# The first 25 microseconds of a four-layer kernel: first tile's mean by halves, transposes reordered, third tile turned by DMA

## The chip, the cores and the metric

The kernel runs on one core of one Trainium2 chip. The metric is the device time of one execution in microseconds (us); lower is better. The kernel before takes 1623.7 us (median of 6 runs).

## The reference

Four layers in turn, A, B, A, B. Only the start of the first one matters here: a layer norm of `x` (2048 x 1024, bf16), then the key, query and value projections.

```python
def _layernorm(x, axis=-1, eps=1e-5):
    m = jnp.mean(x, axis=axis, keepdims=True)
    v = jnp.var(x, axis=axis, keepdims=True)
    return (x - m) / jnp.sqrt(v + eps)
# layer A (cut): qkv = layernorm(x) @ wqkv; linear attention; @ wo; residual
# layer B (cut): ((layernorm(x) @ w_gate) * (layernorm(x) @ w_up)) @ w_down; residual
```

## The kernel before

Rows of `x` are 16 tiles of 128. A tile is centred (the division by the deviation comes later, as the `scale` of an exponential and a relu), transposed so that its 1024 features lie on the partitions, and multiplied with eight slices (128 features each) of the key weights. In the opening, two tiles advance together through the slices as these arrive. A "slice" below is such a piece of weights, 256 KB, as large as a tile of `x`. PE is the engine of matmuls, DVE the vector engine, ACT the scalar engine. To turn a tile is to transpose it, and to evict it is to copy it out of PSUM, where PE has written it.

```python
for c in range(2):                                   # tile 0 in two halves
    load(X[:, 0, c * NB:(c + 1) * NB], x_view[:, 0, c * NB:(c + 1) * NB])
load_x(1)
for k in range(2):    load_k(k, k + 1)               # slices 0, 1
load_x(2)
for k in range(2, 4): load_k(k, k + 1)
load_x(3)
for k in range(4, 8): load_k(k, k + 1)
# ... cut ...
nc.vector.memset(xT[3][:, 0, :], 0.0)
def idle(n):          # n dummy matmuls, 128x512, that keep PE active before data is there
    for _ in range(n):
        nc.tensor.matmul(out=zps[:, 0, :], lhsT=xT[3][:, 0, 0:P], rhs=xT[3][:, 0, :], start=True, stop=True)
# ... cut ...
idle(9)
ln_stats(0)                                          # two bn_stats and an aggregate on DVE
centre(0, stat[0][0][:, 0:1])
nc.scalar.activation(out=junk[:], in_=X[:, 1, :], func=ACT.Copy, scale=1.0 / D, accum_out=mean1[:])
turn_pe(0, 2)                                        # transposes on PE, in two PSUM tiles
take(nc.vector.tensor_copy, 0, 0, 0, 2)              # evict what the first matmul needs
take(nc.scalar.copy, 0, 1, 2, 8)
centre(1, mean1[:])
k_part(0, 0, 1)                                      # tile 0, slice 0: two matmuls
turn_pe(1, 4)
take(nc.vector.tensor_copy, 1, 0, 0, 4)
take(nc.scalar.copy, 1, 1, 4, 8)
ln_stats(2)
centre(2, stat[2][0][:, 0:1])
k_part(1, 0, 1)
for k in range(1, 3):
    for t in range(2): k_part(t, k, k + 1)
turn_pe(2, 8)                                        # tile 2: eight transposes on PE
for t in range(2): k_part(t, 3, 4)
take(nc.scalar.copy, 2, 0, 0, 8)
ln_stats(3); centre(3, stat[3][0][:, 0:1])
turn(XN[:, 3, :], 0, 3)                              # tile 3: turned by DMA
load_q()                                             # query weights, then tiles 4 to 15
# ... cut: the remaining slices of tiles 0 to 2, tile 3, then the queries
```

## Time and profile before

| | before |
|---|---|
| device time, median of 6 | 1623.7 us |
| device time of the traced execution | 1624.31 us |
| PE busy share of the span | 99% |
| named waits of PE, whole run | 2.3 us |
| exponential of tile 3 starts (tiles 0 to 3 done on PE) | 22.20 us |

The page of the profile, its first lines:

```profile
span 1622.4 us, 18054 instructions
PE 1609.2 (99%) x7718; PEld 735.2 (45%) x7869; DVE 615.5 (38%) x941; ACT 283.8 (17%) x383; POOL 54.5 (3%) x135
```

PE does 99% of the span; only what PE does, or waits for, can matter. The view of waits, for PE, shows what it waited for, in us:

```profile
PE ps L168 <- DVE xT L163: 1.2, 1, 1.2
PE pt L411 <- DVE R L398: 0.4, 1, 0.4
PE ps L198 <- DMA W<-in_A_wqkv_dram: 0.4, 1, 0.4
PE ps L198 <- DVE xT L414: 0.3, 1, 0.3
```

A listed wait is counted from the modelled end of the matmul before it, so it can be shorter than the time that PE loses. The last line, 0.3 us for the eviction of tile 1's turn, is a stop of 0.52 us from start to start (7.64 to 8.16, by the single records of the trace), where the transposes before it start 0.056 us apart: about 0.46 us lost.

All of them fall in the first 8.2 us, as the timeline of PE shows (start, length, engine, line, operation, count, and the idle time before with what ended it):

```profile
1.17 4.02 PE L168 MATMUL ps<-xT 128*128 128x512 bf16 x9 [1.17 <-DVE xT L163]
5.17 0.68 PE L411 MATMUL pt<-ident,R 128*128 128x128 bf16 x8
6.23 0.59 PE L198 MATMUL ps<-W,xT 128*128 128x512 bf16 x2 [0.38 <-DMA W<-in_A_wqkv_dram]
7.24 0.62 PE L411 MATMUL pt<-ident,R 128*128 128x128 bf16 x8 [0.42 <-DVE R L398]
8.16 2.33 PE L198 MATMUL ps<-W,xT 128*128 128x512 bf16 x10 [0.30 <-DVE xT L414]
10.33 0.61 PE L411 MATMUL pt<-ident,R 128*128 128x128 bf16 x8
10.77 13.54 PE L198 MATMUL ps<-W,xT 128*128 128x512 bf16 x60
```

The nine dummies take 4.02 us, 0.425 apart: half clock. Then come tile 0's transposes, its first slice, tile 1's transposes, ten matmuls, tile 2's transposes, and a stream without gaps, 0.219 us for a 128x512 matmul. The lengths overlap a little, since matmuls are pipelined; the chain has the occupied time. These are its pieces from 1.65 on (start, length, what):

```profile
1.65 3.85 DMA X<-in_A_x_dram
...
5.51 1.16 ACT junk L422 x2
...
6.70 0.50 DVE R L398
...
8.16 2.33 PE ps L198 x10
10.49 0.45 PE pt L411 x8
```

The chain goes through the load of tile 1, which landed at 5.49 us, and its mean on ACT; and tile 2's transposes hold PE for 0.45 us. The exponential of tile 3:

```profile
22.20 1.11 ACT L203 ACTIVATE e<-ps,rstd 128x1024 bf16<-128x1024 f32 x1
```

### The profile page before, as it was taken

What the parts mean: (1) busy time and instruction counts of PE and PEld (TensorE: products, weight loads), DVE (VectorE), ACT (ScalarE), POOL (GpSimd) and SP (SyncE); (2) the same over time, 40 slices, a digit from 0 to 9 for tenths busy, and PEclk for the clock granted to TensorE, in tenths of its full rate; (3) what the DMA queues carried; (4) which work ended last, traced back from release to release, by engine and by line L of the source; (5) the groups of instructions that cost most, each with busy time, mean ns of one, the idle gap of its engine ahead of it and who ended that gap; (6) DMA issues with size and microseconds to landing.
All of it is one profiled execution on the core that took longest, in us unless ns stands there. A gap on an engine that the chain in (4) does not pass through costs nothing.

```text
span 1622.4 us, 18054 instructions
## 1 busy us (share of the span) xinstructions
PE 1609.2 (99%) x7718; PEld 735.2 (45%) x7869; DVE 615.5 (38%) x941; ACT 283.8 (17%) x383; POOL 54.5 (3%) x135
## 2 busy tenths in 40 slices
PE   9999999999999999999999999999999999999999
PEld 4444444444444444444444444444444444444444
DVE  6799853212311321243245798432123113211111
ACT  5523201101110110011045222011011101101110
POOL 2100000000000000010000000000000000000000
PEclk9999999999999999999999999999999999999999
DMA  7324856511650452142420349555235406511400
GB/s 233 59 72 98 241 162 175 162 53 55 167 168 0 141 160 89 52 155 63 90 56 1 78 98 252 156 163 163 71 101 172 130 20 175 162 65 65 156 0 26
DMA packets 235775, 182.84 MB, mean 113 GB/s; under 512 B 101296, under 2 KB 216496, under 8 KB 235696
## 3 DMA queue, kind: packets, MB, share of 16 engines
q1 hardware_dynamic: 235696, 181.69, 38.9%
q8 instruction: 61, 1.00, 0.3%
q14 instruction: 18, 0.15, 0.0%
HBM read 153.09 MB, written 4.19 MB: 97 GB/s over the span
## 4 chain that ended last, share of the span: by engine, by line
PE 99%; issue 1%; DMA 0%; DVE 0%; ACT 0%; SPq 0%
PE ps L198 50%; PE ps L529 47%; PE ps L556 1%; PE kv L312 0%; DMA X<-in_A_x_dram 0%; PE pm L337 0%; ACT junk L422 0%; PE pt L411 0%; SPq L109 0%; DVE R L398 0%; DVE xT L414 0%; DVE X L537 0%; PE ps L337 0%
## 5 line engine op out<-in xcount | busy, mean ns | idle before, releaser
L529 PE MATMUL ps<-xT,R 128*128 128x512 bf16 x2380 | 525.8, 379 | 2.8
L529 PEld LDWEIGHTS <-R 128*128 128x128 bf16 x2432 | 237.9, 98 | 287.0
L533 DVE TENSOR_TENSOR R<-gs,ps 128x512 bf16<-128x512 f32 x224 | 154.0, 687 | 533.4 <-ACT gs L532 533.4
L198 PEld LDWEIGHTS <-R 128*128 128x128 bf16 x2248 | 220.0, 98 | 265.2
L532 ACT COPY gs<-ps 128x512 f32<-128x512 f32 x224 | 131.3, 586 | 1040.2 <-PE ps L529 1017.2
L529 PE MATMUL ps<-xT,W 128*128 128x512 bf16 x1134 | 250.6, 379 | 0.9
L198 PEld LDWEIGHTS <-xT 128*128 128x128 bf16 x1536 | 149.2, 98 | 180.6 <-issue 2.1
L198 PE MATMUL ps<-W,xT 128*128 128x512 bf16 x996 | 223.1, 379 | 2.3 <-DMA W<-in_A_wqkv_dram 0.4
L529 PEld LDWEIGHTS <-W 128*128 128x128 bf16 x1152 | 112.7, 98 | 135.9
L198 PE MATMUL ps<-W,R 128*128 128x512 bf16 x732 | 170.1, 379 | 0.8
L537 DVE TENSOR_TENSOR X<-X,ps 128x1024 bf16<-128x1024 bf16 (+3 forms) x34 | 39.4, 1159 | 335.7 <-PE ps L198 282.6
L198 PE MATMUL ps<-PQ,R 128*128 128x512 bf16 x486 | 111.6, 379 | 0.6
L198 PE MATMUL ps<-R,R 128*128 128x512 bf16 x506 | 111.8, 379 | 0.4
L198 PE MATMUL ps<-R,xT 128*128 128x512 bf16 x502 | 110.3, 379 | 0.5
L177 DVE BATCH_NORM_STATS2 st<-X 128x6 f32<-128x512 bf16 x128 | 81.9, 682 | 2.1 <-DMA X<-in_A_x_dram 1.9
L203 ACT ACTIVATE e<-ps 128x1024 bf16<-128x1024 f32 x56 | 57.4, 1025 | 140.2 <-PE ps L198 134.7
L181 POOL TENSOR_SCALAR ve<-mv 128x1 f32<-128x1 f32 x64 | 16.8, 262 | 1328.1 <-DVE mv L179 1328.1
L198 PE MATMUL ps<-GL,R 128*128 128x512 bf16 x241 | 57.6, 379 | 0.2
L198 PE MATMUL ps<-xT,R 128*128 128x512 bf16 x240 | 57.5, 379 | 0.2
L382 DVE TENSOR_TENSOR X<-X,ps 128x1024 bf16<-128x1024 bf16 x32 | 38.5, 1212 | 25.5 <-PE ps L198 25.5
L188 DVE TENSOR_SCALAR R<-X,mv,rstd 128x1024 bf16<-128x1024 bf16 x64 | 33.9, 542 | 24.0 <-POOL rstd L183 24.0
L207 DVE TENSOR_SCALAR e<-e 128x1024 bf16<-128x1024 bf16 x64 | 27.0, 422 | 40.0 <-ACT e L203 40.0
(65 smaller groups left out, 446.6 us busy)
## 6 DMA issues: line engine op xcount, KB each, us to landing
R<-in_B_w_gate_dram SPq DMA_DIRECT2D x38, 1024.0 KB, 5.5
R<-in_B_w_up_dram SPq DMA_DIRECT2D x38, 1024.0 KB, 7.4
W<-in_B_w_gate_dram SPq DMA_DIRECT2D x18, 1024.0 KB, 5.4
W<-in_B_w_up_dram SPq DMA_DIRECT2D x18, 1024.0 KB, 7.3
W<-in_A_wqkv_dram SPq DMA_DIRECT2D x10, 1024.0 KB, 6.0
W<-in_B_w_down_dram SPq DMA_DIRECT2D x6, 1024.0 KB, 11.1
PQ<-in_B_w_down_dram SPq DMA_DIRECT2D x4, 1024.0 KB, 7.9
X<-in_A_x_dram SPq DMA_DIRECT2D x15, 256.0 KB, 6.3
```

The source lines that it names most:

```text
L177: nc.vector.bn_stats(out=st[:, c, :], in_=X[:, t, c * NB:(c + 1) * NB])
L181: nc.gpsimd.tensor_scalar(out=ve[:], in0=mv[:, 1:2], scalar1=1e-5, scalar2=None, op0=ALU.add)
L188: nc.vector.tensor_scalar(out=dst, in0=X[:, t, :], scalar1=mv[:, 0:1], scalar2=rstd[:], op0=ALU.subtract, op1=ALU.mult)
L198: nc.tensor.matmul(out=ps[:, n, :], lhsT=lhsT, rhs=rhs[:, n * NB:(n + 1) * NB], start=start, stop=stop)
L203: nc.scalar.activation(out=e[:], in_=flat(ps), func=ACT.Exp, **sc)
L207: nc.vector.tensor_scalar(out=e[:], in0=e[:], scalar1=1.0, scalar2=EPS, op0=ALU.min, op1=ALU.add)
L382: nc.vector.tensor_tensor(out=X[:, t, :], in0=X[:, t, :], in1=flat(ps), op=ALU.add)
L529: nc.tensor.matmul(out=ps[:, n, :], lhsT=w[:, k, j * P:(j + 1) * P], rhs=xT[g % 2][:, k, :], start=(k == 0), stop=(k == KD - 1))
L532: nc.scalar.copy(out=gs[:], in_=ps[:, 0, :])
L533: nc.vector.tensor_tensor(out=hT[:, f, :], in0=gs[:], in1=ps[:, 1, :], op=ALU.mult)
L537: nc.vector.tensor_tensor(out=X[:, t, a:b], in0=X[:, t, a:b], in1=ps, op=ALU.add)
L556: nc.tensor.matmul(out=ps[:, 0, 0:b - a], lhsT=hT[:, f, tl * P:(tl + 1) * P], rhs=wd[f][:, a:b], start=(f == 0), stop=(f == KF - 1))
```

## The change

Its intent: shorten the way to the first transposes (half of tile 0's mean on ACT, half on DVE, in place of bn_stats), let tile 0's slice 1 run while tile 1's turn is evicted (its transposes go ahead of that slice), and take tile 2's transposes off PE by turning that tile by DMA, as tile 3 already was. The loads are put in the order in which they are now needed, and the dummies read a constant, so that they need not wait for a memset.

```diff
-    for c in range(2):
-        load(X[:, 0, c * NB:(c + 1) * NB], x_view[:, 0, c * NB:(c + 1) * NB])
+    load_x(0)
     load_x(1)
-    for k in range(2):
+    for k in range(0, 3):
         load_k(k, k + 1)
     load_x(2)
-    for k in range(2, 4):
-        load_k(k, k + 1)
+    load_k(3, 4)
     load_x(3)
 ... cut
-    nc.vector.memset(xT[3][:, 0, :], 0.0)
 ... cut: idle() reads nc.const_aps.tensor(1.0, ...) for both operands
+            def mean_by_halves(t, i):
+                nc.scalar.activation(out=junk[:, 0:NB], in_=X[:, t, 0:NB], func=ACT.Copy, scale=1.0 / D,
+                                     accum_out=part[:, i:i + 1])
+                nc.vector.tensor_scalar(out=junk[:, NB:D], in0=X[:, t, NB:D], scalar1=1.0 / D, scalar2=0.0,
+                                        op0=ALU.mult, op1=ALU.add, accum_out=part[:, i + 1:i + 2])
 ... cut: centre_by_halves subtracts both parts in one DVE instruction
             idle(9)
-            ln_stats(0)
-            centre(0, stat[0][0][:, 0:1])
+            mean_by_halves(0, 0)
+            centre_by_halves(0, 0)
 ... cut
-            ln_stats(2)
-            centre(2, stat[2][0][:, 0:1])
-            k_part(1, 0, 1)
-            for k in range(1, 3):
-                for t in range(2):
-                    k_part(t, k, k + 1)
-            turn_pe(2, 8)
-            for t in range(2):
-                k_part(t, 3, 4)
-            take(nc.scalar.copy, 2, 0, 0, 8)
+            k_part(0, 1, 2)
+            k_part(1, 0, 2)
+            for t in range(2):
+                k_part(t, 2, 3)
+            mean_by_halves(2, 2)
+            centre_by_halves(2, 2)
+            turn(XN[:, 2, :], 0, 2)
             ln_stats(3)
             centre(3, stat[3][0][:, 0:1])
             turn(XN[:, 3, :], 0, 3)
 ... cut: ln_stats(0), (1), (2) follow here; then slices 3 to 7 of tiles 0 and 1, tile 2 whole, tile 3 whole
```

More of the change, by code (lines that the diff above doesn't have):

```diff
@@ L167, in idle @@
         for _ in range(n):
-            nc.tensor.matmul(out=zps[:, 0, :], lhsT=xT[3][:, 0, 0:P], rhs=xT[3][:, 0, :], start=True, stop=True)
+            nc.tensor.matmul(out=zps[:, 0, :], lhsT=nc.const_aps.tensor(1.0, [P, P], BF16),
+                             rhs=nc.const_aps.tensor(1.0, [P, NB], BF16), start=True, stop=True)
     stat = {}
@@ L400, in layer_A, with turn_pe, centre_by_halves @@
             pts = {}
-            def turn_pe(t, cut):
-                for h, (i, j) in enumerate(((0, cut), (cut, KD))):
-                    if i == j:
-                        continue
-                    tag, bufs = ("mm", 3) if h else ("kv0", 1)
-                    pt = psum.tile([P, KD, P], BF16, tag=tag, bufs=bufs, name="pt")
-                    pts[t, h] = pt
-                    for k in range(i, j):
-                        nc.tensor.transpose(out=pt[:, k, :], in_=XN[:, t, k * P:(k + 1) * P], identity=ident[:])
+            def turn_pe(t, h, a, b):
+                tag, bufs = ("mm", 3) if t and h else (f"kv{h}", 1)
+                pts[t, h] = psum.tile([P, KD, P], BF16, tag=tag, bufs=bufs, name="pt")
+                for k in range(a, b):
+                    nc.tensor.transpose(out=pts[t, h][:, k, :], in_=XN[:, t, k * P:(k + 1) * P], identity=ident[:])
             def take(copy, t, h, a, b):
                 copy(out=xT[0][:, a:b, t * P:(t + 1) * P], in_=pts[t, h][:, a:b, :])
+            part = small.tile([P, 4], F32, tag="part", bufs=1, name="part")
             mean1 = small.tile([P, 1], F32, tag="mean1", bufs=1, name="mean1")
             junk = small.tile([P, D], BF16, tag="eb", bufs=3, name="junk")
+            def mean_by_halves(t, i):
[3 more added lines that the diff above has]
+                                        op0=ALU.mult, op1=ALU.add, accum_out=part[:, i + 1:i + 2])
+            def centre_by_halves(t, i):
+                nc.vector.tensor_scalar(out=XN[:, t, :], in0=X[:, t, :], scalar1=part[:, i:i + 1],
+                                        scalar2=part[:, i + 1:i + 2], op0=ALU.subtract, op1=ALU.subtract)
             idle(9)
-            ln_stats(0)
-            centre(0, stat[0][0][:, 0:1])
+            mean_by_halves(0, 0)
+            centre_by_halves(0, 0)
             nc.scalar.activation(out=junk[:], in_=X[:, 1, :], func=ACT.Copy, scale=1.0 / D, accum_out=mean1[:])
-            turn_pe(0, 2)
+            turn_pe(0, 0, 0, 2)
             take(nc.vector.tensor_copy, 0, 0, 0, 2)
+            turn_pe(0, 1, 2, 8)
             take(nc.scalar.copy, 0, 1, 2, 8)
@@ L427, in layer_A @@
             k_part(0, 0, 1)
-            turn_pe(1, 4)
+            turn_pe(1, 0, 0, 4)
             take(nc.vector.tensor_copy, 1, 0, 0, 4)
+            turn_pe(1, 1, 4, 8)
             take(nc.scalar.copy, 1, 1, 4, 8)
-            ln_stats(2)
-            centre(2, stat[2][0][:, 0:1])
-            k_part(1, 0, 1)
-            for k in range(1, 3):
-                for t in range(2):
-                    k_part(t, k, k + 1)
-            turn_pe(2, 8)
+            k_part(0, 1, 2)
+            k_part(1, 0, 2)
             for t in range(2):
-                k_part(t, 3, 4)
-            take(nc.scalar.copy, 2, 0, 0, 8)
+                k_part(t, 2, 3)
+            mean_by_halves(2, 2)
+            centre_by_halves(2, 2)
+            turn(XN[:, 2, :], 0, 2)
             ln_stats(3)
@@ L446, in layer_A @@
                 load_x(t)
-            ln_stats(1)
+            for t in range(3):
+                ln_stats(t)
+            for k in range(3, 6):
+                for t in range(2):
+                    k_part(t, k, k + 1)
             for t in range(2):
-                k_part(t, 4, 6)
-            k_part(0, 6, 8)
-            k_part(2, 0, 6)
-            for t in range(1, 3):
                 k_part(t, 6, 8)
+            k_part(2, 0, 8)
             k_part(3, 0, 8)
```

## The prediction

> **What bounds the kernel now.** The page's busy row gives PE 1609.2 us of a 1622.4 us span (99%); the chain of waits is 99% PE. The waits list gives PE about 2.3 us of named waits in the whole run, all before 8.2 us. The change touches the first 25 us, so within 2% is all but certain; the question is sign and size below 0.2%.
>
> **The opening before (timeline).** Nine dummy matmuls run at half clock (425 ns each) until 5.19. Tile 0's first half lands at 3.04; bn_stats (1.28), aggregate (0.21), centre (0.49); its transposes start at 5.17. Tile 1 lands at 5.49 (the chain follows it), ACT mean 1.16, centre 0.50, transposes at 7.24, DVE copy 0.43, and from 8.16 PE runs without a gap at 0.219 us per matmul (10.74 us for 49). Tile 2's eight transposes cost 0.45. By 10.77 PE has done 12 of the 32 matmuls of tiles 0 and 1. The 64 matmuls of tiles 0 to 3 end near 22.2, where the queries begin.
>
> **What the change does.**
> - Tile 0's mean in two parallel halves: ACT's is an estimate from the 1024-wide one (1.06 + 0.19), about 0.75; with centre, 1.3 after landing instead of 2.0. The whole tile lands later than its first half did (estimate 3.0 to 3.6). Its transposes move from 5.17 to about 4.7, where the dummies, freed of the 0.27 memset, end. Worth little alone: PE next waits for tile 1 and weights.
> - Loads: one issue fewer; weight slice 2 ahead of tile 2. Pieces of 256 KB land 0.6 to 0.7 us apart: slice 2 at about 7.9 (was 8.59), tile 2 at 8.6, slices 3 to 7 as before at 9.3, 10.6, 11.4, 12.0, 12.6.
> - Tile 2's turn leaves PE (0.45 saved). Its DMA turn is issued at about 9.9 and queues behind slice 7. Tile 3's turn before took 1.2 us to its first packet, 1.5 us of packets, and landed 3.1 us after issue; so tile 2 lands about 14.0, tile 3 about 15.5, the query weights about 0.4 after their 22.14.
> - PE order: tile 0's second slice and tile 1's first two before slice 2.
>
> **Critical path.** Weight slices feed PE: slice 4 at about 10.6, then 16 matmuls, so tiles 0 and 1 end at about 14.1. Before, equal work ended at 10.77 + 20 x 0.219 = 15.15. Gain 1.0 us, less 0 to 0.4 waiting for tile 2's turned data (wanted 14.1, there 14.0 to 14.4), plus up to 0.4 if tile 1 and the slices land earlier. Later bounds have slack: phi of tile 0 ends near 16.6, its PSUM is wanted near 17.7; the query weights' second half is wanted near 23, there near 22.6. After that PE has no gaps, so the gain reaches the end.
>
> The Trainium skill, "TensorE: Matmul & The Clock Gate", on the HAM clock gate, says full clock comes after about 3.4 us of sustained work, in a free-running window. The trace agrees: clock raised at 5.33 us, 4.2 us after the first matmul. With PE waiting for data, a shift of it costs little.
>
> **Prediction:** 1622.8 us, 1621.9 to 1623.7 in 8 of 10. Faster by over 2%: 0.003; within: 0.992; slower: 0.005.
>
> **What would show it.** Tile 0's transposes near 4.7; none of tile 2 on PE; PE waits on slices 3 or 4 between 9.4 and 10.6; tile 2's turned block landing near 14; first query matmul near 21.3 instead of 22.4.
>
> **What would make it wrong.** Tile 2's turn landing past 15; the slow first packets (about 0.5 us, seen at tile 1's start) falling on tile 0; the clock rising a window later because PE is sparser from 5 to 7 us; query weights late.

## The result, and the profile after

| | before | after |
|---|---|---|
| device time, median of 6 | 1623.7 us | 1623.13 us |
| lowest to highest | 1623.1 to 1624.11 | 1622.72 to 1623.35 |
| device time of the traced execution | 1624.31 us | 1622.72 us |
| exponential of tile 3 starts, in that trace | 22.20 us | 20.62 us |

The ratio is 0.9996, with a 95% interval of 0.9984 to 1.0009: the same, within 2%. A ratio is the mean time of one kernel's runs over the mean of the other's in the same rounds, so it is not quite the ratio of the medians. The medians differ by 0.57 us.

The two traces differ by more: 1.6 us of device time. The trace of before is of an execution slower than all its 6 timed ones, and that of after is the fastest of its 6. About 1 us of what a reader sees between these two traces is therefore chance.

The page after, the waits of PE, and its timeline:

```profile
span 1620.9 us, 18201 instructions
PE 1617.2 (100%) x7861; PEld 735.1 (45%) x7861; DVE 616.3 (38%) x944; ACT 284.0 (18%) x386; POOL 54.2 (3%) x135
```

```profile
PE ps L165 <- PEq L633: 0.8, 1, 0.8
PE pt L405 <- DVE R L421: 0.2, 1, 0.2
```

```profile
0.76 4.00 PE L165 MATMUL ps<-const-bfloat16-1.0 128*128 128x512 bf16 x9 [0.76 <-PEq L633]
4.92 1.04 PE L405 MATMUL pt<-ident,R 128*128 128x128 bf16 x8 [0.16 <-DVE R L421]
5.74 0.98 PE L196 MATMUL ps<-W,xT 128*128 128x512 bf16 x2
6.56 0.61 PE L405 MATMUL pt<-ident,R 128*128 128x128 bf16 x8
7.00 17.25 PE L196 MATMUL ps<-W,xT 128*128 128x512 bf16 x79
```

The dummies start 0.41 us earlier; after them PE waits only 0.16 us, and tile 2's transposes are gone. The stop for tile 1's eviction is gone too: the last of its transposes starts at 6.95 and the next matmul, of tile 0's slice 1, at 7.00. The busy sums of PE are not to be compared between the two pages: the trace of before lacks some matmul records (7718 of PE's instructions against 7861, while the change took only eight away). The first pieces of the chain after:

```profile
0.72 2.75 DMA X<-in_A_x_dram
...
3.50 0.71 DVE junk L417 x2
...
4.31 0.56 DVE R L421
...
4.92 1.04 PE pt L405 x8
5.95 0.77 PE ps L196 x2
6.72 0.45 PE pt L405 x8
7.17 52.92 PE ps L196 x245
```

The chain now runs through tile 0 and then stays on PE. The matmuls and transposes up to 6.5 us run at half clock (tile 0's transposes start 0.107 us apart, tile 1's 0.056; the 1.04 us of the chain also has the whole length of one of them, so it is not to be set beside the 0.45). In this execution the trace's clock record rises at 6.51 us; in the first trace of before, at 5.33. The exponential of tile 3:

```profile
20.62 1.11 ACT L201 ACTIVATE e<-ps,rstd 128x1024 bf16<-128x1024 f32 x1 [0.91 <-PE ps L196]
```

One check makes everything that follows simpler. The span less the start of tile 3's exponential is 1622.4 - 22.20 = 1600.2 us before and 1620.9 - 20.62 = 1600.3 us after. It is between 1600.1 and 1600.4 us in all fourteen traces. So whatever differs between these kernels, and between the traced executions of one kernel, has happened before tile 3's exponential, and that start can stand for the whole time.

### The profile page after: what moved, and what is told of

The parts are those of the page before. It is cut to its first block, busy times and chain, and to the rows that moved or that the text cites. A ratio compares the mean times of both kernels' runs of the same rounds, so it can differ in the third digit from the quotient of the medians.

```text
span 1620.9 us, 18201 instructions
## 1 busy us (share of the span) xinstructions
PE 1617.2 (100%) x7861; PEld 735.1 (45%) x7861; DVE 616.3 (38%) x944; ACT 284.0 (18%) x386; POOL 54.2 (3%) x135
## 4 chain that ended last, share of the span: by engine, by line
PE 100%; DMA 0%; DVE 0%; issue 0%; DVEq 0%
PE ps L196 50%; PE ps L534 48%; PE ps L561 1%; PE kv L310 0%; PE pm L335 0%; DMA X<-in_A_x_dram 0%; PE pt L405 0%; DVE junk L417 0%; DVE R L421 0%; DVE X L542 0%; PE ps L335 0%; DVEq L421 0%
```

## The experiments

All were timed in 5 rounds, each beside 9 runs of the kernel before. A difference below is the mean of the kernel's 5 runs less the mean of those 9. One kernel's runs spread with a standard deviation of 0.2 to 0.5 us (e_bn0_b 0.89, e_gap 0.74), so a difference is good to 0.3 to 0.5 us, and for those two to no better than 0.7. The four runs that end in _b were on one chip, the other eight on another; each is compared with the kernel before on its own chip.

| run | what it is | difference, us | runs, us |
|---|---|---|---|
| c_before | before, unchanged | +0.23 | 1623.22 to 1624.29 |
| c_after | after, unchanged | -0.61 | 1622.54 to 1623.19 |
| e_loads_only | before, new loads | +0.50 | 1623.83 to 1624.58 |
| e_loads_back | after, old loads | -0.69 | 1622.35 to 1623.44 |
| e_turn2_pe_b | after, tile 2 on PE | -0.22 | 1623.19 to 1623.69 |
| e_turn2_only_b | before, tile 2 by DMA | -0.42 | 1623.04 to 1623.63 |
| e_halves_only_b | before, tile 0 by halves | +0.16 | 1623.56 to 1624.16 |
| e_bn0_b | after, tile 0 by bn_stats | +0.17 | 1622.79 to 1624.78 |
| e_bn0_fill | the same, 11 dummies | -0.72 | 1622.75 to 1623.35 |
| e_gap | after, 6 dummies | +0.15 | 1622.74 to 1624.67 |
| v_x3_late | a version | -0.77 | 1622.41 to 1623.4 |
| v_split | a version | -0.90 | 1622.44 to 1623.24 |

### c_before and c_after: how much of the traces' difference is chance

No edit.

> The kernel before, unchanged: a control of how far one kernel differs from itself. Its first trace had tile 1's load land at 5.49 us (four fifths of a microsecond behind its bytes, with first packets of 0.5 to 1.0 us) and the exponential of tile 3 start at 22.20. Theory A (that late landing belongs to the kernel's load order and shapes): tile 1 lands again at 5.3 to 5.6 and tile 3's exponential starts at 22.0 to 22.4. Rival B (it was chance, and half of the 1.5 us between the two traces was luck of single executions): tile 1 lands at 4.2 to 4.8 and tile 3's exponential starts at 21.2 to 21.8. Both: ratio to before 1.0000 within 0.0003, times 1623.1 to 1624.3.

> The changed kernel, unchanged: more runs than the six on record. Theory A: 1.0 to 1.6 us less than before (ratio 0.9990 to 0.9994), tile 1 lands at 4.0 to 4.3, tile 3's exponential starts at 20.4 to 21.2 with no wait of PE for a DMA. Rival B: ratio 0.9996 to 0.9998, 0.3 to 0.7 us. [...] each us of half clock after 5 should cost 0.5 us here, as PE never waits.

The control differs from itself by 0.23 us, two fifths of the difference of medians that is to be explained: 0.3 us is taken below as the floor. The changed kernel is 0.61 us below before; its slowest run (1623.19) lies above only one of the nine of before (1623.14). The times are those of rival B. The control's trace, of its fastest execution:

```profile
1.17 3.49 PE L168 MATMUL ps<-xT 128*128 128x512 bf16 x9 [1.17 <-DVE xT L163]
5.11 0.62 PE L411 MATMUL pt<-ident,R 128*128 128x128 bf16 x8 [0.44 <-DVE R L398]
5.78 0.60 PE L198 MATMUL ps<-W,xT 128*128 128x512 bf16 x2
6.22 0.61 PE L411 MATMUL pt<-ident,R 128*128 128x128 bf16 x8
7.13 2.33 PE L198 MATMUL ps<-W,xT 128*128 128x512 bf16 x10 [0.30 <-DVE xT L414]
9.30 0.61 PE L411 MATMUL pt<-ident,R 128*128 128x128 bf16 x8
9.74 14.62 PE L198 MATMUL ps<-W,xT 128*128 128x512 bf16 x65
```

Tile 1 landed at 4.42 us here, not 5.49, the ten matmuls begin at 7.13 instead of 8.16, and tile 3's exponential starts at 21.17. So one kernel's opening moves by a whole microsecond between two executions, by when one 256 KB load lands. The fourteen traces together show more than this pair: with tile 0 loaded in halves tile 1 landed anywhere from 4.42 to 5.49 us (seven traces), with tile 0 as one piece always between 3.97 and 4.11 (seven traces). So the late landing was chance in one execution, but the spread goes with the load order, as theory A had said in part. The first weight slice lands no earlier for it: 5.35 to 6.19 us in the one order, 5.11 to 6.15 in the other. The trace of c_after ends its opening at 20.74, only 0.43 us earlier than the control's, and shows a wait that the first trace of after did not have:

```profile
6.52 3.37 PE L196 MATMUL ps<-W,xT 128*128 128x512 bf16 x14
10.18 14.19 PE L196 MATMUL ps<-W,xT 128*128 128x512 bf16 x63 [0.29 <-DMA W<-in_A_wqkv_dram]
```

That is slice 4, which landed at 10.13 us. From start to start the stop is 0.67 us (9.51 to 10.18) in place of 0.22, and slice 3, which landed at 8.82, cost another 0.15 (8.50 to 8.87) that no list names: 0.60 us lost in all. In the first trace of after slice 4 landed at 9.72, and PE, slower to get there with the late clock, did not wait.

### e_loads_only and e_loads_back: the load order

```diff
 e_loads_only: the kernel before, with load_x(0); load_x(1); slices 0, 1, 2; load_x(2); slice 3; load_x(3); ...
 e_loads_back: the changed kernel, with tile 0 in halves, tile 1, slices 0, 1, tile 2, slices 2, 3, tile 3, ...
```

> The kernel before with the new load order alone (tile 0 in one piece, slice 2 ahead of tile 2). If tile 1's earlier landing is what pays: tile 1 lands near 4.1, its transposes on PE move from 7.24 to about 6.1, tile 3's exponential starts 0.7 to 1.1 us before c_before's, time 0.6 to 1.0 us less. If the loads are worth nothing by themselves (PE order, statistics and the turn of tile 2 pay): within 0.3 us of c_before.

> The changed kernel with the old load order (tile 0 in halves, tile 2 ahead of slice 2). If the loads pay: tile 1 lands near 5.4, PE waits about 1 us for it, and tile 3's exponential starts 0.7 to 1.1 us after c_after's. If they do not: within 0.3 us of c_after.

The loads do not pay in either direction. Alone they cost 0.50 us against the runs of before, and 0.27 against c_before, the measure that the expectation named (the second is within the floor). In the trace tile 0 as one piece landed at 3.45 us where its first half had landed at 2.98, bn_stats begin with that half, and tile 0's transposes moved from 5.11 to 5.58, tile 3's exponential from 21.17 to 21.64. In the changed kernel the old loads do as well as the new (-0.69 against -0.61), and its first transposes start at 4.72 us instead of 4.85 (c_after).

### e_turn2_pe_b and e_turn2_only_b: tile 2's transposes

```diff
 e_turn2_pe: the changed kernel
-            turn(XN[:, 2, :], 0, 2)
+            turn_pe(2, 0, 0, 8)
+            take(nc.scalar.copy, 2, 0, 0, 8)
 e_turn2_only: the kernel before
-            turn_pe(2, 8)
+            turn(XN[:, 2, :], 0, 2)
             for t in range(2):
                 k_part(t, 3, 4)
-            take(nc.scalar.copy, 2, 0, 0, 8)
 ... and tile 2's matmuls after the last of tile 1
```

> The changed kernel, but tile 2 is transposed on PE again, between weight slices 2 and 3, and evicted by ACT. Theory A (the gain is mostly PE work taken away: eight transposes, 0.44 us in both traces of before, and PE is the limit): tile 3's exponential starts 0.4 to 0.5 us after c_after's 20.74 and the time goes up by 0.3 to 0.5 us, to about 1623.4, most of the gain gone. Rival C (slice 4's landing is the limit, as c_after's wait of 0.29 us for it says): the transposes fill the wait, cost 0.0 to 0.2 us, and PE shows no wait for slice 4.

> The kernel before with tile 2's turn by DMA alone (and tile 2's matmuls after all of tile 1's). Theory A: PE loses eight transposes of 0.44 us and nothing waits: 0.4 to 0.5 us less than before, that is nearly the whole change. Rival C: PE comes 0.44 us earlier to slices 4 and 5, and waits for one of them; gain 0.0 to 0.3.

By itself, the DMA turn of tile 2 gives 0.42 us, which is what the eight transposes hold PE for (0.45 us in the chain). The traces settle it against rival C better than times that are good to 0.3 us:

```profile
7.84 16.36 PE L198 MATMUL ps<-W,xT 128*128 128x512 bf16 x73 [0.30 <-DVE xT L414]
21.44 1.11 ACT L203 ACTIVATE e<-ps,rstd 128x1024 bf16<-128x1024 f32 x1 [1.27 <-PE ps L198]
```

From the start of the stream (7.84; in the two traces of before 8.16 and 7.13) to tile 3's exponential takes 13.60 us here and 14.04 in both traces of before: 0.44 less, whatever the loads did earlier, and PE waits for no slice on the way. Undone, the DMA turn takes 0.39 us from the gain (-0.22 against -0.61, measured on two chips). Both directions agree with theory A. The trace of e_turn2_pe_b shows more than the transposes, though:

```profile
6.93 2.36 PE L196 MATMUL ps<-W,xT 128*128 128x512 bf16 x10
9.68 0.62 PE L405 MATMUL pt<-ident,R 128*128 128x128 bf16 x8 [0.39 <-DVE R L421]
10.14 14.19 PE L196 MATMUL ps<-W,xT 128*128 128x512 bf16 x63
```

PE waits 0.39 us for tile 2 to be centred, since the new load order puts tile 2 behind slice 2 (it landed at 8.23; at 6.99 in c_before). Tile 3's exponential starts at 21.56, 0.82 us after c_after's and not 0.4 to 0.5. Part of this experiment's loss is therefore that wait, in an order not made for it; e_turn2_only_b is the cleaner of the two.

### e_halves_only_b and e_bn0_b: tile 0's mean by halves

```diff
 e_halves_only: the kernel before
-            ln_stats(0)
-            centre(0, stat[0][0][:, 0:1])
+            mean_by_halves(0, 0)
+            centre_by_halves(0, 0)
 ... and ln_stats(0) ahead of ln_stats(1)
 e_bn0: the changed kernel, the reverse
```

> The kernel before with tile 0's mean by halves alone. Theory B: 0.3 to 0.5 us less than before. Rival D (in the kernel before tile 1's mean on ACT is what PE waits for next, so tile 0's part is worth nothing there): tile 0's transposes move from 5.1 to about 4.6, tile 1's stay near 6.2, and the time is within 0.15 us of before.

> The changed kernel with tile 0's mean from bn_stats again. Theory B (the gain is mostly the shorter chain to tile 0's transposes): they start at 5.5 instead of 4.9, and tile 3's exponential starts 0.4 to 0.6 us later than c_after's; the time goes up by 0.4 to 0.6 us. Rival C (slice 4 is the limit): up by 0.0 to 0.3, and the wait for slice 4 vanishes.

Alone, the half means give nothing (+0.16, within the floor). That is the number of rival D, but the trace is no clean case of it: tile 0 was centred at 4.69, yet its transposes started at 4.99 and not 4.6, since the nine dummies, at half clock, held PE until then; and tile 1 landed at 4.92 in this execution, so its transposes started at 6.75 and not 6.2. Taken away from the changed kernel, they did something that neither theory had said. The five runs were 1622.79, 1623.09, 1624.31, 1624.47 and 1624.78: two as fast as the changed kernel, three slower by more than a microsecond, and none between. The standard deviation, 0.89 us, is about twice the largest so far (0.46). The one traced is the fastest. It starts tile 0's transposes 0.74 us later than c_after and still reaches tile 3's exponential at 20.77, against 20.74:

```profile
0.76 3.45 PE L165 MATMUL ps<-const-bfloat16-1.0 128*128 128x512 bf16 x9 [0.76 <-PEq L633]
5.59 0.62 PE L405 MATMUL pt<-ident,R 128*128 128x128 bf16 x8 [1.38 <-DVE R L396]
```

So the later transposes are not what costs: c_after, which is earlier, loses 0.60 us to slices 3 and 4, and here PE comes when they have landed (8.78 and 10.13). What stands out is PE idle for 1.38 us after the dummies.

### e_bn0_fill and e_gap: the idle time before the first transposes

```diff
 e_bn0_fill: e_bn0 with
-            idle(9)
+            idle(11)
 e_gap: the changed kernel with
-            idle(9)
+            idle(6)
```

> e_bn0 (the changed kernel with tile 0's mean from bn_stats) with 11 dummy matmuls instead of 9. e_bn0_b's five runs fell into two groups, 1622.8 to 1623.1 and 1624.3 to 1624.8; its profiled one, a fast one, had PE idle for 1.38 us between the dummies and tile 0's transposes, with the clock already raised at 3.5 us. Theory E (in the slow ones that idle gap made the clock rise a window later, about 3.4 us, at half a microsecond lost for each): with the gap filled the slow group goes, all five within 1622.8 to 1623.7. Rival F (the groups come from the later chain or the DMA): still runs above 1624.2.

> The changed kernel, half means and all, with 6 dummies instead of 9: they end near 3.3 and PE idles about 1.5 us before tile 0's transposes at 4.9. No work on the chain is longer. Theory E: slow runs appear, 1.0 to 1.8 us above c_after's 1622.94, so that some are at 1624.0 or more. Rival F: within 0.2 us of c_after, none above 1623.5.

Two more dummies, which do no work, take e_bn0 from +0.17 to -0.72 us: the slow group is gone (1622.75 to 1623.35). Three fewer dummies in the changed kernel, with the work otherwise untouched, bring one: 1622.74, 1623.82, 1624.12, 1624.38, 1624.67. The traced execution of e_gap is again the fast one:

```profile
0.76 2.72 PE L165 MATMUL ps<-const-bfloat16-1.0 128*128 128x512 bf16 x6 [0.76 <-PEq L633]
4.78 0.62 PE L405 MATMUL pt<-ident,R 128*128 128x128 bf16 x8 [1.30 <-DVE R L421]
```

Its wait of 1.30 us costs it nothing: its tile 3 starts its exponential at 20.66. It is shown that an idle PE before the first transposes makes slow executions (e_gap against c_after, same chip, four of five against none) and, with less weight, that filling it removes them (e_bn0_fill ran on another chip than e_bn0_b). That the clock is the way from one to the other (rising a window later) is argued, not shown: no slow execution was traced. Three observations fit. In both fast traces the clock had risen before the transposes (3.52 and 4.20 us in the clock records). The clock moves in steps: of the twelve traces with a clock record, eight have it up for 1617.92 us and the four with the latest rises (5.96 to 7.19 us) for 1614.50, which is 3.42 us less. And the loss of 1.1 to 2.0 us against each kernel's fastest run is about what half clock over one more window would cost: the Trainium skill, "TensorE: Matmul & The Clock Gate", section "What's actually happening", gives a free-running window of 3.4 us, and half of that, 1.7 us, is my estimate from the page.

### v_x3_late and v_split: two versions

```diff
 v_x3_late: e_loads_back with
-    load_x(3)
-    for k in range(4, 8):
+    load_k(4, 5)
+    load_x(3)
+    for k in range(5, 8):
 v_split: v_x3_late with tile 0 centred in columns 0:256, then 256:1024, and idle(8)
```

> A version meant to be faster: the changed kernel with tile 0 loaded in halves and tile 2 ahead of slice 2 (as in e_loads_back) and slice 4 ahead of tile 3, so that the wait for slice 4 seen in c_after goes. Slice 4 lands near 9.3 instead of 10.1. If that wait matters in most runs: 0.15 to 0.3 us below e_loads_back, about 1622.6 mean. If it was rare: the same as e_loads_back, 1622.86 within 0.2.

> v_x3_late with tile 0 centred in two pieces (256 columns, then 768) and 8 dummies: transposes start near 4.4 instead of 4.7. If PE is the limit throughout: 0.1 to 0.3 us below v_x3_late. If the clock rises later for the shorter dummy stretch (Theory E), some runs are above 1623.5.

The differences, -0.77 and -0.90, are not clear of the changed kernel's -0.61, of e_loads_back's -0.69 or of e_bn0_fill's -0.72. The aim was missed in the trace: slice 4 landed at 10.18 and 9.75, not at 9.3, because slice 2 landed 1.77 and 1.50 us behind tile 2 in these two executions, where it was 0.6 to 0.9 in the other five traces with that order, and v_split's PE still waited twice for weights (0.20 and 0.16 us). With 8 dummies PE was idle for 0.25 us before the transposes and the clock rose at 5.98; no run was above 1623.24, so the slow runs that theory E allowed for did not come. These five beat the kernel before by more than the floor; which of them is best is not settled.

## Why the prediction was right or wrong

The prediction was 1622.8 us with a range of 1621.9 to 1623.7; 1623.13 was measured, within the range. Its forecast gain was 0.9 us and the measured one is 0.57 to 0.61.

- **"Worth little alone" (tile 0's mean by halves): right.** e_halves_only_b gave +0.16, and e_bn0_fill does without the half means at -0.72. Their one measured use is that PE is not idle for long between nine dummies and the first transposes, and more dummies do that as well. Size of the half mean: predicted 0.75 us, measured 0.73 on ACT (3.50 to 4.23).
- **"Tile 2's turn leaves PE (0.45 saved)": right,** and it is most of the gain: 0.42 us alone, 0.44 by the traces.
- **"Gain 1.0 us" (15.15 less 14.1): the mis-sized term.** Both numbers were too late, for one reason: they come from one execution whose loads were late (slice 4 at 10.64, in the control at 9.70). The 15.15 was read from one execution in which tile 1 landed at 5.49; by the control's trace the same work ended at 9.74 + 20 x 0.219 = 14.12. The first trace's execution was slower than all six timed ones of its kernel, and its 1624.31 us against the 1623.5 to 1624.11 of the three timed runs then at hand could have told so before predicting. The 14.1 counted slice 4 at 10.6; it landed at 9.72 and 10.13, and the exponential of tile 3 less its last 32 matmuls gives 20.62 - 32 x 0.219 = 13.6 and 20.74 - 7.0 = 13.7. But the control's trace is the fastest of its five. An estimate for a typical execution moves each end by its trace's distance from the median of its kernel: about 14.6 before (15.15 - 0.61 and 14.12 + 0.60) and 13.8 to 14.0 after. The two errors partly cancel, since they share a cause; that so little was left of them is luck.
- **PE waiting for slices 3 or 4: half right.** Seen in c_after (0.60 us from start to start) and not in the first trace of after, whose clock rose later and whose slice 4 landed 0.41 us earlier.
- **"PE order": named, but given no size, and no experiment changes it alone.** The traces show what it removes, the stop of about 0.46 us for tile 1's eviction, which is in both traces of before and in neither of after. Waits for slices 3 and 4 can take it back, as in c_after.
- **Waiting for tile 2's turned data (0 to 0.4): did not happen.** It landed at 12.93 and 13.20 us, not 14.0, and tile 3's at 14.28 and 14.72, not 15.5. PE wanted tile 2's near 13.7.
- **Tile 0's transposes near 4.7, first query matmul near 21.3:** 4.92 and 4.85; about 20.6.
- **"With PE waiting for data, a shift of [the clock] costs little": not contradicted for the kernel as it is, wrong as a rule.** With a rise at 6.51 us the first trace of after ended its opening 0.12 us before c_after, whose transposes change to full spacing near 5.2 but which waited for slices; two executions do not separate these. But e_gap and e_bn0_b lose up to 2.0 us between their own executions from an idle PE, which the prediction named as a danger ("PE is sparser") and then gave no size.

What stays open: the clock in a slow execution of e_gap or e_bn0_b was not seen; and the remaining 0.2 us of the gain, beside tile 2's turn, is below the floor and was not divided among the earlier dummies, the order on PE and the half means.

## What to carry to other kernels

A trace is one execution: before a gain is computed from its arrival times, compare that execution's own time with the kernel's timed runs, and take a second trace when the effect sought is as small as their spread. Where an engine is busy to the end, work taken off it is worth its own length (0.45 us of transposes gave 0.42), while a shorter chain towards the next wait may be worth nothing. Dummy work at the start should last until real work comes: two dummies more removed a slow group of over a microsecond, and three fewer brought it. How long an idle stretch is harmless was not measured: 0.92 us in the trace of e_loads_only came with no separate slow group.

## What the Trainium skill lacked or had wrong

- "TensorE: Matmul & The Clock Gate", section "What's actually happening", has full clock after at least one busy window of about 3.4 us. Here the clock record rises 2.76 to 6.0 us after the first dummy (0.76 to 3.52 us in e_bn0_b, 1.17 to 4.00 in c_before, 0.76 to 6.51 in the first trace of after, 1.18 to 7.19 in e_halves_only_b): a rise after less than a window is possible, so a window need not be busy throughout. In e_gap the dummies had ended 0.7 us before the clock rose, at 4.20.
- The same page says that the ramp is under 1% of a typical span and that one should not fit a specific count of slow matmuls. That holds (at most 2 us of 1623), but it lacks that an idle stretch of 1.3 us within the ramp splits executions into two groups over a microsecond apart (e_gap; e_bn0_b, 1.38 us), which spoils comparisons of small changes.
- The same page, section "Part 4: PE-mode transpose", gives about 390 ns for a 128x128 transpose in isolation and about 275 ns in a kernel. These are lengths of one; for a row of them the spacing counts: here eight held PE for 0.45 us, 56 ns each, at full clock, and started 107 ns apart while the clock was low (first trace of after).
- "DMA: Bandwidth & Descriptors", section "Anatomy of one DMA", has a fixed part of about 2 us for a DMA (by another issue path). The first load agrees: 2.3 us from issue to landing for 128 KB. The page has nothing on the spread: the same 256 KB load of tile 1 in the same kernel landed at 4.42 and at 5.49 us in two executions; it was 3.97 to 4.11 us in all seven traces with tile 0 loaded as one piece before it.
